# The opening of a fused attention and expert kernel: sums of squares on other engines, larger pieces, two more weight blocks converted early

## The chip, the core and the metric

The kernel runs on one core of a Trainium2 chip. What counts is the device time of one execution in microseconds, from the first to the last thing the core does. The engines are named as in the profile: PE (TensorE), DVE (VectorE), ACT (ScalarE), POOL (GpSimd) and SP (SyncE, which here only issues transfers).

## The reference

Two batches of 6016 tokens with 256 channels go through a channel attention and two dense layers. The scores contract over the tokens, so each batch has one 256 x 256 score matrix:

```python
qn = q / (np.linalg.norm(q, axis=1, keepdims=True) + 1e-06)   # norm over the 6016 tokens
kn = k / (np.linalg.norm(k, axis=1, keepdims=True) + 1e-06)
s = kn.transpose(0, 2, 1) @ qn / tau
a = softmax(s)                                                # with 1e-09 in the denominator
x = (v @ a).reshape(12032, 256)
x = (sigmoid(x @ w_gate) * (x @ w_val)) @ w_out               # d_ff 1536
h = x @ w_in
out = (h - np.tanh(h)) @ w_out2                               # d_ff 2048
```

All inputs are fp32, the weights arrive as float64 bit patterns in two 32-bit words each (seen from the kernel), and the products are done on TensorE in fp32 (S) or as pairs of fp32r halves, high and low, with three products for one.

## The kernel before

**Order of the whole.** The schedule is written out by hand: each engine executes its instructions in the order in which the Python text emits them. The opening handles batch 0's q and k, the softmax and the first weight blocks; then a list of units (24 tiles of up to 512 tokens, two layers) keeps PE busy to the end, with batch 1's scores done beside it. Only the opening is touched by the change.

**Pieces.** Each partition holds 47 rows (tokens) of q and k. `pieces` cuts them: three of 2 rows, nine of 4, then 2, 2 and 1. `qk_load` (L215) puts one transfer for q and one for k on SP's queue, into a ring of 14 buffers, so seven pieces can be in flight; the loop (L357) loads piece j + 6, then works on piece j.

**Scores and squares.** `qk_scores` (L249) multiplies each row of k, in two halves of 128 channels, with the row of q, and accumulates in one PSUM bank, S0; each product in fp32 shows as two PE instructions. `qk_squares` (L239) squares a piece on ACT into an SBUF buffer (two of these in turn) and adds it on DVE to a sum of four rows for q and one for k. `fold` (L245) adds halves of the sums until one row is left. Then PE forms the norms (`nps`, L383), a chain of small DVE and ACT steps takes the roots and inverses, PE spreads q's inverse norms over the partitions (`spread`, L403), DVE scales the scores (L276), ACT takes the exponentials (L280), and PE transposes (`turn`, L289). PE has S products of the last pieces (their second half, c = 1) behind nps, and products of batch 1 (`fill`, L232, loaded by `fill_load`, L223), to do in between.

**Weights.** Weight blocks are named wgv{f}_{jc} and wo{c}; one is 512 KB of float64 words. `convert` (L102) is a generator that turns them into fp32r halves in five steps: `load` on SP, `rebias` (L118) on ACT, `shift` (L124) and `join` (L130) on DVE, `hi` (L137) on ACT, `lo` (L142) on DVE. `join(n)` also issues load(n + ahead). `pump(n)` advances it by n yields, and so sets where its instructions stand among the others. The first stream, conv0, has two items with ahead=2: both loads are issued among the first pieces, and the steps run in the pumps of j = 5 to 7. The second stream, conv, has ahead=4 and starts at j = 9. The order of the steps is this (L149):

```python
        for n in range(lead):
            rebias(n)
        for n in range(len(items) + 2):
            if shift(n):
                yield
            ...
            for do in (lambda n: lo(n - 2), join):
                if do(n):
                    yield
            hi(n)
            if lead == 2:
                rebias(n + 2)
```

**Products of the weights.** `aw_block` (L294) multiplies a converted block with the softmax; its first use of wgv1 and wgv2 is between the first units. `ones0` is a tile of ones; `warm` products on it stand ahead of S on PE (L350).

Of the kernel before, what the change touches and what calls it, by code (L numbers as in the profile page):

```python
# [8 lines left out]
F32 = mybir.dt.float32  # L9
# [4 lines left out]
AF = mybir.ActivationFunctionType  # L14
# [3 lines left out]
P = 128  # L18
B, S, D = 2, 6016, 256
R = S // P  # L20
RP = 4
# [13 lines left out]
LATE = 8  # L35


NRAW, NYQ, WARM = 14, 1, 3


START2, DENSE = 24.3, 0.48
# [23 lines left out]
def attn_moe_kernel(  # L65
# [12 lines left out]
    nc = tc.nc  # L78
    ctx.enter_context(tc.manual_schedule())
    mm = nc.tensor.matmul  # L80
# [6 lines left out]
    sp = sctx.enter_context(tc.tile_pool(name="sp", bufs=1, reuse_waits="tile"))  # L87
# [3 lines left out]
    def ring(name):  # L91
        return pp.tile([P, CH], F32, tag="ring", bufs=4, name=name)

    def bank(tag, name):
        return pp.tile([P, CH], F32, tag=tag, name=name)
# [6 lines left out]
    def convert(pool, items, done, ahead=4, raws=4, lead=2):  # L102

        jobs = {}

        def load(n):
            if n < len(items):
                src, dst, name = items[n]  # L110
                raw = pool.tile([P, CH, 2], U32, tag="craw", bufs=raws, name=f"raw_{name}")
                nc.sync.dma_start(raw, src.bitcast(U32).rearrange("p (c two) -> p c two", two=2))
                jobs[n] = [raw[:, :, 0], raw[:, :, 1].bitcast(F32), dst, name, None, None]

        def rebias(n):
            if n in jobs:
                x = pool.tile([P, CH], U32, tag="cx", bufs=4, name=f"x_{jobs[n][3]}")
                nc.scalar.activation(x.bitcast(F32), jobs[n][1], AF.Prelu, scale=2.0**-112, alpha=-(2.0**32))  # L118
                jobs[n][4] = x

        def shift(n):
            if n in jobs:
                x = jobs[n][4]
                nc.vector.tensor_scalar(x, x, 3, 0xFFFFFFFF, op0=ALU.logical_shift_left, op1=ALU.bitwise_and)  # L124
                return True

        def join(n):
            if n in jobs:
                x = jobs[n][4]
                nc.vector.scalar_tensor_tensor(x, jobs[n][0], 29, x, op0=ALU.logical_shift_right, op1=ALU.bitwise_or)  # L130
                load(n + ahead)
                return True

        def hi(n):
            if n in jobs:
                t = jobs[n][5] = jobs[n][2]()
                nc.scalar.copy(t[:, 0], jobs[n][4].bitcast(F32))  # L137

        def lo(n):
            if n in jobs:  # L140
                _, _, _, name, x, t = jobs.pop(n)
                nc.vector.tensor_sub(t[:, 1], x.bitcast(F32), t[:, 0].bitcast(F32))  # L142
                done(name)
                return True

        for n in range(ahead):
            load(n)
# [6 lines that stand above are left out]
            if lead == 1:  # L154
                rebias(n + 1)
# [6 lines that stand above are left out]
# [3 lines left out]
    def pump(n):  # L165
        for _ in range(n):
            if stream[0] is not None and next(stream[0], 1) == 1:
                stream[0] = None


    ident = base.tile([P, P], F32, name="ident")
    ones0 = sp.tile([P, P], F32, name="ones0")
    sums = [sp.tile([P, RP, D], F32, name=f"sum{x}") for x in "qk"]
    rs = [base.tile([P, 2], F32, name=f"rs{b}") for b in range(B)]
    warm = base.tile([P, 1], F32, name="warm")
# [6 lines left out]
    def constants():  # L182
        for t in sums:
            nc.gpsimd.memset(t, 0.0)
        make_identity(nc, ident)
        nc.vector.memset(c_b, C_B)
        nc.vector.memset(c_m, -U_MAX)
        nc.gpsimd.dma_start(itau, tau.to_broadcast((P, 1)))
# [7 lines left out]
    def wgv_item(f, jc):  # L196
        return (wgv[2 * f + jc], lambda: wgv_t[f][:, :, jc, :], f"wgv{f}_{jc}")
# [1 line left out]
    def wo_item(c):  # L199
        return (wo[c], lambda: wo_t[c], f"wo{c}")  # L200

    conv0 = [wgv_item(0, jc) for jc in range(2)]
    conv = [wgv_item(1, jc) for jc in range(2)]
    for f in range(2, NW // 2):
        conv += [wo_item(f - 2), wgv_item(f, 0), wgv_item(f, 1)]
    conv += [wo_item(c) for c in range(NO - 2, NO)]
# [2 lines left out]
    qk0 = {}  # L209
    S0 = bank("o0", "S0").rearrange("p (c j) -> p c j", c=2)  # L210

    def token_rows(x, b):
        return x[b].rearrange("(p r) c -> p r c", r=R)

    def qk_load(r0, rn):  # L215
        for x, src in (("q", q), ("k", k)):
            raw = qk0[x, r0] = sp.tile([P, RP, D], F32, name=f"raw{x}{r0}", tag="raw", bufs=NRAW)
            nc.sync.dma_start(raw[:, :rn, :], token_rows(src, 0)[:, r0 : r0 + rn, :])
# [4 lines left out]
    def fill_load():  # L223
        fp = fctx.enter_context(tc.tile_pool(name="fp", bufs=1, side="right", reuse_waits="tile"))
        for r0, rn in FILL_LOADS:
            for x, src in (("q", q), ("k", k)):
                t = fp.tile([P, rn, D], F32, name=f"fill{x}{r0}")
                nc.sync.dma_start(t, token_rows(src, 1)[:, r0 : r0 + rn, :])
                for r in range(rn):
                    fq[x, r0 + r] = t[:, r, :]  # L230
# [5 lines left out]
                mm(S1[:, c], fq["k", r][:, c * P : (c + 1) * P], fq["q", r], start=r == 0 and c == 0, stop=r == sum(FILL) - 1, skip_group_check=True)  # L236
        filled[0] += FILL[g]

    def qk_squares(r0, rn):  # L239
        for x, t in zip("qk", sums):  # L240
            sq = sp.tile([P, RP, D], F32, name=f"sq{x}{r0}", tag="sq", bufs=2)[:, :rn, :]
            nc.scalar.activation(sq, qk0[x, r0][:, :rn, :], AF.Square)
            nc.vector.tensor_add(t[:, :rn, :], t[:, :rn, :], sq)

    def fold(h):  # L245
        for t in sums:
            nc.vector.tensor_add(t[:, :h, :], t[:, :h, :], t[:, h : 2 * h, :])

    def qk_scores(r0, rn, cs=(0, 1), rows=None):  # L249
        for r in rows or range(rn):  # L250
            for c in cs:
                w = qk0["k", r0][:, r, c * P : (c + 1) * P]
                mm(S0[:, c], w, qk0["q", r0][:, r, :], start=r0 + r == 0 and c == 0, stop=r0 + r == R - 1, skip_group_check=True)  # L253
# [55 lines left out]
    def load_v(i):  # L309
        if i >= NT:  # L310
            return
        b, off, _, n = tiles[i]
        t = vp.tile([P, 2, NM], F32, tag="vraw", name=f"vraw{i}")
        nc.sync.dma_start(t[:, :, :n], vT[b].rearrange("(c p) n -> p c n", p=P)[:, :, off : off + n])
        raws[i] = t
# [23 lines left out]
        while not ready.issuperset(names):  # L339
            pump(1)  # L340

    pieces = [(r0, 2) for r0 in range(0, 6, 2)] + [(r0, RP) for r0 in range(6, 42, RP)] + [(42, 2), (44, 2), (46, 1)]
    NP = len(pieces)
    AHEAD = NRAW // 2 - 1
    nc.vector.memset(ones0, 1.0)
    qk_load(*pieces[0])
    qk_load(*pieces[1])
    constants()
    for n in range(WARM):
        mm(bank("o1", f"warm{n}")[:, :P], ones0, ones0, start=True, stop=True)  # L350
    for j, pc in enumerate(pieces[2:AHEAD]):
        qk_load(*pc)
        if j == 2:
# [3 lines left out]
    for j, pc in enumerate(pieces[:-1]):  # L357
        if j + AHEAD < NP:
            qk_load(*pieces[j + AHEAD])
            if j + AHEAD == NP - 1:  # L360
                load_v(0)
        if j == NP - 3:
            fold(2)
        qk_squares(*pc)
        if 5 <= j < 8:
            pump(2)
        if j == 9:
            pump(1000)
            stream[0] = convert(stg, conv, stash)
            pump(1)  # L370
            fill_load()
        qk_scores(*pc, (0, 1) if j < NP - 4 else (0,))
        if j == NP - 4:
            qk_scores(*pc, (1,), range(2))
    fold(1)
    qk_squares(*pieces[-1])
    split_v(0, eng=nc.gpsimd)

# [7 lines left out]
    rn = sp.tile([P, 4], F32, name="rn")  # L386
# [5 lines left out]
    dq = sp.tile([P, 2, P], F32, name="dq")  # L392
# [3 lines left out]
    nc.vector.tensor_scalar_mul(rn[:, 2:4], rn[:, 2:4], itau[:, 0:1])  # L396
    pump(2)
    qk_scores(*pieces[-1], (0,))
    qk_scores(*pieces[-4], (1,), range(2, RP))
    for pc in pieces[-3:-1]:  # L400
        qk_scores(*pc, (1,))
    ps = ring("spread")
    mm(ps[:, :D], ones0, dq.rearrange("p c j -> p (c j)"), start=True, stop=True)  # L403
    qk_scores(*pieces[-1], (1,))
    rqs = sp.tile([P, D], F32, name="rqs")
    nc.scalar.copy(rqs, ps[:, :D])
    e0 = sp.tile([P, 2, D], F32, name="e0")
# [332 lines left out]
    for u in units:  # L740
        at, kind, i, c = u
# [4 lines left out]
        if kind == 1 and i == 1 and c == 2:  # L746
            t = cst.tile([P, NM], F32, name="s1_out")
# [86 lines left out]
```

## Time and profile before

| | |
|---|---|
| median of 3 runs | 2316.07 us (2316.01 to 2316.17) |
| the profiled execution's own time | 2316.01 us |
| its span, first to last instruction | 2314.2 us |
| mean granted clock of PE | 1.000 |
| busy share PE, DVE, ACT, POOL | 100%, 79%, 68%, 2% |
| first S product, first nps | 4.34 us, 44.65 us |

The span is what the trace covers; the profiled time has 1.8 us more around it. All times inside the trace are microseconds from the start of the span. The opening is the stretch up to about 62 us, where the units begin.

### The profile page before, as it was taken

The page shows a single profiled execution, that of the slowest core. Times are in us where ns is not written, and L with a number is a line of the kernel's source. Part 1 is how long each engine was busy: PE and PEld are TensorE (multiplying, and loading weights), DVE is VectorE, ACT ScalarE, POOL GpSimd, SP SyncE. Part 2 cuts the span into 40 slices and gives each one's busy share as a digit, 9 for nine tenths or more (in the row PEclk, how much of TensorE's full clock was granted, in tenths as well). Part 3 has the DMA queues.
Part 4 walks back from the last instruction along what each step waited for, and adds up shares of the span by engine and source line. Part 5 has one row for each costly group of instructions (what it writes and reads, how often), then busy time and mean ns, then how long its engine had stood idle before and what let it go on. Part 6 is the DMA issues. An engine that isn't in the chain of part 4 may idle for free.

```text
span 2314.2 us, 28241 instructions
## 1 busy us (share of the span) xinstructions
PE 2302.7 (100%) x10416; PEld 1928.2 (83%) x10416; DVE 1826.2 (79%) x2886; ACT 1578.5 (68%) x2862; POOL 48.3 (2%) x50
## 2 busy tenths in 40 slices
PE   9999999999999999999999999999999999999998
PEld 7888888888888888888888888888888888888897
DVE  7778888888888888877777777777777777777778
ACT  6567777677676767776666666666666666666667
POOL 1000000000000000000000000000000000000006
PEclk9999999999999999999999999999999999999999
DMA  9640001110101101011110000000000000000000
GB/s 367 210 133 9 20 22 37 37 37 19 37 28 32 38 19 37 0 35 37 55 37 12 6 19 10 10 19 1 19 14 5 19 10 10 19 1 17 10 1 17
DMA packets 39242, 84.65 MB, mean 37 GB/s; under 512 B 4032, under 2 KB 17344, under 8 KB 37568
## 3 DMA queue, kind: packets, MB, share of 16 engines
q1 hardware_dynamic: 38064, 76.36, 9.9%
q0 software_dynamic: 896, 6.29, 0.7%
q8 instruction: 81, 1.33, 0.2%
q14 instruction: 57, 0.47, 0.1%
q10 hardware_dynamic: 144, 0.20, 0.0%
HBM read 63.96 MB, written 18.87 MB: 36 GB/s over the span
## 4 chain that ended last, share of the span: by engine, by line
PE 95%; DVE 3%; ACT 1%; DMA 1%; issue 0%; SPq 0%; DVEq 0%; ACTq 0%
PE ps L450 11%; PE ps L449 11%; PE ps L454 11%; PE h L450 7%; PE h L454 7%; PE h L449 7%; PE o L454 7%; PE o L449 7%; PE o L450 7%; PE y L450 5%; PE y L454 5%; PE y L449 5%; PE S L253 1%; DMA rawk<-in_k_dram 1%; PE aw L300 0%
## 5 line engine op out<-in xcount | busy, mean ns | idle before, releaser
L450 PE MATMUL ps<-vhl,aw 128*128 128x512 f32 (+1 forms) x1152 | 443.6, 385 | 0.0
L449 PE MATMUL ps<-vhl,aw 128*128 128x512 f32 (+1 forms) x1152 | 443.3, 385 | 0.0
L516 DVE TENSOR_TENSOR d<-h,d 128x512 f32<-128x512 f32 (+1 forms) x368 | 251.6, 684 | 234.2 <-ACT d L512 233.6
L544 ACT CAST hl<-s 128x512 fp32r<-128x512 f32 (+1 forms) x384 | 234.8, 612 | 279.7 <-DVE s L520 274.0
L511 ACT ACTIVATE u<-h 128x512 f32<-128x512 f32 (+1 forms) x384 | 226.5, 590 | 238.2 <-PE h L454 237.8
L454 PE MATMUL ps<-vhl,aw 128*128 128x512 f32 (+1 forms) x1152 | 349.9, 385 | 0.0
L518 DVE TENSOR_TENSOR u<-h,u 128x512 f32<-128x512 f32 (+1 forms) x360 | 245.7, 683 | 112.3 <-ACT big L515 112.2
L449 PE MATMUL o<-hl,wv 128*128 128x512 f32 (+1 forms) x768 | 295.8, 385 | 1.2 <-ACT hl L544 1.2
L450 PE MATMUL h<-yhl,wi 128*128 128x512 f32 (+1 forms) x768 | 295.8, 385 | 0.0
L449 PE MATMUL h<-yhl,wi 128*128 128x512 f32 (+1 forms) x768 | 295.7, 385 | 0.0
L450 PE MATMUL o<-hl,wv 128*128 128x512 f32 (+1 forms) x768 | 295.5, 385 | 0.0
L520 DVE COPY_PREDICATED s<-big,d 128x512 f32<-128x512 int16 (+1 forms) x368 | 274.9, 747 | 13.1
L513 ACT ACTIVATE s<-u,c_b 128x512 f32<-128x512 f32 (+1 forms) x384 | 275.9, 719 | 1.9 <-DVE hl L546 1.9
L515 ACT ACTIVATE big<-u,c_m 128x512 bf16<-128x512 f32 (+1 forms) x368 | 263.5, 716 | 0.0
L519 DVE SCALAR_TENSOR_TENSOR s<-s,u 128x512 f32<-128x512 f32 (+1 forms) x360 | 247.1, 686 | 12.3
L450 PEld LDWEIGHTS ps<-vhl,aw 128*128 128x128 f32 x1152 | 216.4, 188 | 41.2
L449 PEld LDWEIGHTS ps<-vhl,aw 128*128 128x128 f32 x1152 | 216.3, 188 | 40.9
L454 PEld LDWEIGHTS ps<-vhl,aw 128*128 128x128 f32 x1152 | 215.7, 188 | 41.5
L490 DVE TENSOR_TENSOR sg<-ps,sg 128x512 f32<-128x512 f32 (+1 forms) x288 | 194.4, 675 | 70.6 <-PE ps L454 54.6
L546 DVE TENSOR_TENSOR hl<-s,hl 128x512 fp32r<-128x512 f32 (+1 forms) x361 | 243.8, 675 | 0.6 <-ACT hl L544 0.6
L454 PE MATMUL o<-hl,wv 128*128 128x512 f32 (+1 forms) x768 | 234.8, 387 | 2.2 <-POOL hl L546 1.7
L489 ACT ACTIVATE sg<-ps 128x512 f32<-128x512 f32 (+1 forms) x288 | 170.0, 590 | 98.2 <-PE ps L454 93.7
(157 smaller groups left out, 3530.6 us busy)
## 6 DMA issues: line engine op xcount, KB each, us to landing
vraw<-in_vT_dram SPq DMA_DIRECT2D x22, 512.0 KB, 3.7
out_dram<-out SPq DMA_DIRECT2D x44, 256.0 KB, 2.2
raw_wgv<-in_wgv_dram SPq DMA_DIRECT2D x12, 512.0 KB, 5.8
wgv_d<-wgv POOLq DMA_DIRECT2D x6, 1024.0 KB, 6.8
wb<-wgv_d SPq DMA_DIRECT2D x6, 1024.0 KB, 4.8
raw<-in_q_dram SPq DMA_DIRECT2D x47, 128.0 KB, 2.1
raw<-in_k_dram SPq DMA_DIRECT2D x47, 128.0 KB, 2.2
rawq<-in_q_dram SPq DMA_DIRECT2D x9, 512.0 KB, 10.2
```

Source lines behind the costliest of these rows:

```text
L449: mm(ps[:, :n], wh, xh, start=first and j == 0, stop=False)
L450: mm(ps[:, :n], wl, xh, start=False, stop=False)
L454: mm(ps[:, :n], wh, xl, start=False, stop=last and j == len(wts) - 1)
L511: nc.scalar.activation(u, H, AF.Square)
L513: nc.scalar.activation(s, u, AF.Square, scale=C_S, bias=c_b[:, 0:1])
L515: nc.scalar.activation(big, u, AF.Relu, bias=c_m[:, 0:1])
L516: nc.vector.tensor_sub(d, H, d)
L518: nc.vector.tensor_mul(w, H, u)
L519: nc.vector.scalar_tensor_tensor(s, s, C_D, w, op0=ALU.add, op1=ALU.mult)
L520: nc.vector.copy_predicated(s, big.bitcast(I16), d)
L544: nc.scalar.copy(hl[:, 0, :n], x)
L546: eng.tensor_sub(hl[:, 1, :n], x, hl[:, 0, :n].bitcast(F32))
```

## The change

- `qk_squares` gets an argument `away`. For pieces 0 to 7 (QPOOL) q's squares stay in SBUF and are added on GpSimd. All other squares are done in steps of two rows, written by ACT to a PSUM bank of the common ring of four, and added from there on DVE.
- The pieces are now one of 2 rows, ten of 4, then 2, 2 and 1: 14 in all.
- conv0 has four items, wgv0 and wgv1, and conv begins with wo0. conv0 is still opened with ahead=2. The pumps of two yields now run at j = 5 to 9, and what is left of conv0 at j = 10.
- `fill_load` comes ahead of the second stream's first loads.
- The products on constants are four of 256 columns ahead of S, and three more after piece 0 (before: three of 128 columns ahead of S). `ones0` is twice as wide.
- The second half (c = 1) of all four rows of the fourth piece from the end goes behind nps (before: two of them), and behind the spread product stand the last two pieces instead of one.

```diff
--- before.py
+++ after.py
@@ -35,7 +35,8 @@
 LATE = 8
 
 
-NRAW, NYQ, WARM = 14, 1, 3
+NRAW, NYQ, WARM = 14, 1, (4, 3)
+QPOOL = 8
 
 
 START2, DENSE = 24.3, 0.48
@@ -169,7 +170,7 @@
 
 
     ident = base.tile([P, P], F32, name="ident")
-    ones0 = sp.tile([P, P], F32, name="ones0")
+    ones0 = sp.tile([P, D], F32, name="ones0")
     sums = [sp.tile([P, RP, D], F32, name=f"sum{x}") for x in "qk"]
     rs = [base.tile([P, 2], F32, name=f"rs{b}") for b in range(B)]
     warm = base.tile([P, 1], F32, name="warm")
@@ -199,8 +200,8 @@
     def wo_item(c):
         return (wo[c], lambda: wo_t[c], f"wo{c}")
 
-    conv0 = [wgv_item(0, jc) for jc in range(2)]
-    conv = [wgv_item(1, jc) for jc in range(2)]
+    conv0 = [wgv_item(f, jc) for f in range(2) for jc in range(2)]
+    conv = []
     for f in range(2, NW // 2):
         conv += [wo_item(f - 2), wgv_item(f, 0), wgv_item(f, 1)]
     conv += [wo_item(c) for c in range(NO - 2, NO)]
@@ -236,11 +237,19 @@
                 mm(S1[:, c], fq["k", r][:, c * P : (c + 1) * P], fq["q", r], start=r == 0 and c == 0, stop=r == sum(FILL) - 1, skip_group_check=True)
         filled[0] += FILL[g]
 
-    def qk_squares(r0, rn):
+    def qk_squares(r0, rn, away=False):
         for x, t in zip("qk", sums):
-            sq = sp.tile([P, RP, D], F32, name=f"sq{x}{r0}", tag="sq", bufs=2)[:, :rn, :]
-            nc.scalar.activation(sq, qk0[x, r0][:, :rn, :], AF.Square)
-            nc.vector.tensor_add(t[:, :rn, :], t[:, :rn, :], sq)
+            raw = qk0[x, r0]
+            if x == "q" and away:
+                sq = sp.tile([P, RP, D], F32, name=f"sq{x}{r0}", tag="sq", bufs=2)[:, :rn, :]
+                nc.scalar.activation(sq, raw[:, :rn, :], AF.Square)
+                nc.gpsimd.tensor_add(t[:, :rn, :], t[:, :rn, :], sq)
+                continue
+            for r in range(0, rn, 2):
+                rs_ = slice(r, min(rn, r + 2))
+                sq = ring(f"sq{x}{r0}_{r}").rearrange("p (r c) -> p r c", c=D)[:, : rs_.stop - r, :]
+                nc.scalar.activation(sq, raw[:, rs_, :], AF.Square)
+                nc.vector.tensor_add(t[:, rs_, :], t[:, rs_, :], sq)
 
     def fold(h):
         for t in sums:
@@ -339,15 +348,19 @@
         while not ready.issuperset(names):
             pump(1)
 
-    pieces = [(r0, 2) for r0 in range(0, 6, 2)] + [(r0, RP) for r0 in range(6, 42, RP)] + [(42, 2), (44, 2), (46, 1)]
+    pieces = [(0, 2)] + [(r0, RP) for r0 in range(2, 42, RP)] + [(42, 2), (44, 2), (46, 1)]
     NP = len(pieces)
     AHEAD = NRAW // 2 - 1
     nc.vector.memset(ones0, 1.0)
     qk_load(*pieces[0])
     qk_load(*pieces[1])
     constants()
-    for n in range(WARM):
-        mm(bank("o1", f"warm{n}")[:, :P], ones0, ones0, start=True, stop=True)
+
+    def warm_up(h):
+        for n in range(WARM[h]):
+            mm(bank("o1", f"warm{h}_{n}")[:, :D], ones0[:, :P], ones0, start=True, stop=True)
+
+    warm_up(0)
     for j, pc in enumerate(pieces[2:AHEAD]):
         qk_load(*pc)
         if j == 2:
@@ -361,17 +374,17 @@
                 load_v(0)
         if j == NP - 3:
             fold(2)
-        qk_squares(*pc)
-        if 5 <= j < 8:
+        qk_squares(*pc, j < QPOOL)
+        if 5 <= j < 10:
             pump(2)
-        if j == 9:
+        if j == 10:
             pump(1000)
+            fill_load()
             stream[0] = convert(stg, conv, stash)
             pump(1)
-            fill_load()
         qk_scores(*pc, (0, 1) if j < NP - 4 else (0,))
-        if j == NP - 4:
-            qk_scores(*pc, (1,), range(2))
+        if j == 0:
+            warm_up(1)
     fold(1)
     qk_squares(*pieces[-1])
     split_v(0, eng=nc.gpsimd)
@@ -396,12 +409,12 @@
     nc.vector.tensor_scalar_mul(rn[:, 2:4], rn[:, 2:4], itau[:, 0:1])
     pump(2)
     qk_scores(*pieces[-1], (0,))
-    qk_scores(*pieces[-4], (1,), range(2, RP))
-    for pc in pieces[-3:-1]:
+    for pc in pieces[-4:-2]:
         qk_scores(*pc, (1,))
     ps = ring("spread")
-    mm(ps[:, :D], ones0, dq.rearrange("p c j -> p (c j)"), start=True, stop=True)
-    qk_scores(*pieces[-1], (1,))
+    mm(ps[:, :D], ones0[:, :P], dq.rearrange("p c j -> p (c j)"), start=True, stop=True)
+    for pc in pieces[-2:]:
+        qk_scores(*pc, (1,))
     rqs = sp.tile([P, D], F32, name="rqs")
     nc.scalar.copy(rqs, ps[:, :D])
     e0 = sp.tile([P, 2, D], F32, name="e0")
```

## Rows read from the trace of the kernel before

**Rows 1.** The page's head and part 1: busy us, share, instructions.

```profile
span 2314.2 us, 28241 instructions
...
PE 2302.7 (100%) x10416; PEld 1928.2 (83%) x10416; DVE 1826.2 (79%) x2886; ACT 1578.5 (68%) x2862; POOL 48.3 (2%) x50
```

**Rows 2.** Windows over the opening: us; busy us (instructions) of PE, PEld, DVE, ACT, POOL; PEclk; DMA share; GB/s.

```profile
30.00:40.00 10.00, 10.00 (x48) 8.81 (x47) 10.00 (x10) 7.60 (x8) 0.00 (x0) 1.00 1.04 387
```

**Rows 3.** PE in order of time: start, us, what, xcount, idle before and its releaser.

```profile
4.34 14.66 PE L253 MATMUL S<-rawq,rawk 128*128 128x256 f32 x56 [0.79 <-DMA rawk<-in_k_dram]
19.54 25.27 PE L253 MATMUL S<-rawq,rawk 128*128 128x256 f32 x116 [0.54 <-DMA rawk<-in_k_dram]
44.65 0.50 PE L383 MATMUL nps<-ones,sumq 128*128 128x2 f32 x4
45.02 0.59 PE L383 MATMUL nps<-ones,sumk 128*128 128x2 f32 x4
```

**Rows 4.** Windows of the S products on PE: us, busy (instructions), PEclk, DMA share, GB/s.

```profile
4.50:8.50 4.00, 4.00 (x10) 1.00 0.71 237
...
20.00:40.00 20.00, 20.00 (x94) 1.00 1.03 398
```

**Rows 5.** ACT in order of time.

```profile
4.23 0.63 ACT L242 ACTIVATE sqk<-rawk 128x512 f32<-128x512 f32 x1
...
8.79 0.63 ACT L242 ACTIVATE sqk<-rawk 128x512 f32<-128x512 f32 x1 [0.32 <-DMA rawk<-in_k_dram]
...
19.49 1.06 ACT L242 ACTIVATE sqk<-rawk 128x1024 f32<-128x1024 f32 x1 [0.22 <-DMA rawk<-in_k_dram]
20.45 1.23 ACT L118 ACTIVATE x_wgv<-raw_wgv 128x512 f32<-128x512 f32 x2
21.58 1.04 ACT L242 ACTIVATE sqq<-rawq 128x1024 f32<-128x1024 f32 x1
22.53 1.04 ACT L242 ACTIVATE sqk<-rawk 128x1024 f32<-128x1024 f32 x1
```

**Rows 6.** SP's queue in order of time: start and length of the issue.

```profile
5.86 2.07 SPq L112 DMA_DIRECT2D raw_wgv<-in_wgv_dram  x2
...
18.20 0.33 SPq L218 DMA_DIRECT2D rawq<-in_q_dram  x1
...
28.44 0.33 SPq L218 DMA_DIRECT2D rawq<-in_q_dram  x1
```

**Rows 7.** DVE in order of time.

```profile
43.38 0.42 DVE L243 TENSOR_TENSOR sumq<-sumq,sqq 128x256 f32<-128x256 f32 x1
43.71 0.41 DVE L243 TENSOR_TENSOR sumk<-sumk,sqk 128x256 f32<-128x256 f32 x1
...
65.82 0.69 DVE L490 TENSOR_TENSOR sg<-ps,sg 128x512 f32<-128x512 f32 x1 [0.80 <-ACT sg L489]
66.43 0.68 DVE L130 SCALAR_TENSOR_TENSOR x_wgv<-raw_wgv,x_wgv 128x512 uint32<-128x512 uint32 x1
67.03 0.42 DVE L124 TENSOR_SCALAR x_wo<-x_wo 128x512 uint32<-128x512 uint32 x1
67.36 0.69 DVE L142 TENSOR_TENSOR wgv<-x_wgv,wgv 128x512 fp32r<-128x512 f32 x1
```

**Rows 8.** GpSimd and DVE in order of time, and the page's usual duration.

```profile
43.83 2.65 POOL L100 TENSOR_TENSOR vhl<-vraw,vhl 128x512 fp32r<-128x512 f32 x2 [40.03 <-ACT vhl L99]
...
2266.63 1.29 POOL L546 TENSOR_TENSOR hl<-s,hl 128x512 fp32r<-128x512 f32 x1 [3.12 <-PE h L450]
...
2267.10 1.42 DVE L520 COPY_PREDICATED s<-big,d 128x512 f32<-128x512 int16 x1
...
L520 DVE COPY_PREDICATED s<-big,d 128x512 f32<-128x512 int16 (+1 forms) x368 | 274.9, 747 | 13.1
```

**Rows 9.** PE before the second turn, and PE's waits for conversions (total, times, longest).

```profile
52.19 0.44 PE L289 MATMUL turn<-ident,e 128*128 128x128 f32 x2 [0.35 <-ACT e L280]
...
PE aw L300 <- DVE wgv L142: 1.0, 2, 0.6
```

## The prediction

> **What bounds the kernel now.** I read the page first. TensorE (PE) is busy 2302.7 of 2314.2 us [rows 1], so time can only be won where PE waits or runs slowly, and only lost where it is made to wait. The change edits the opening alone, so I went there by ten-microsecond windows, then through PE, ACT, SP and DVE in order of time.
>
> PE starts the products S at 4.34. The first 56 instructions take 14.66 us, the next 116 take 25.27 us without a gap, and the norm products nps begin at 44.65, directly behind them [rows 3]. The pace changes on the way: ten instructions in 4 us at first, 94 in 20 us later, so 0.43 us each and then 0.21 to 0.22 us [rows 4]. The granted clock reads 1.00 in both stretches, but the pace is that of 1.2 and of 2.4 GHz.
>
> DVE is just as full: 10.00 of 10 us between 30 and 40, with the DMA engines at a share of 1.04 [rows 2]. Its last sum ends at 43.71 + 0.41 = 44.12 [rows 7], half a microsecond before PE asks for it. So three things run level in the opening: the transfers, the sums of squares on DVE, and PE. Whatever makes the sums late by more than half a microsecond moves nps, and with it all that follows.
>
> The transfers come in the order in which SP issues them. The two weight loads are issued at 5.86, behind fourteen rows of q and k [rows 6]; the fifth piece after them lands at 19.49 [rows 5], and PE waits 0.54 us for it [rows 3]. From 18.20 to 28.44 SP can issue only once in 1.28 us [rows 6], whenever one of the 512 KB transfers ahead has drained: 0.64 us for one row of q with its k (256 KB).
>
> **What the change can win.** The 56 first instructions at the fast pace are 12.2 us, not 14.66; with the waits of 0.54, of 0.35 before the second turn, and of 1.0 in two places for the conversion of a weight block [rows 9], all that can be had in the opening is 2.5 + 0.5 + 0.4 + 1.0 = 4.4 us, 0.19% of the kernel. 0.2% (4.6 us) is about what a measurement of this kernel can tell from no change.
>
> **Where it loses: the third weight block.** The converter still runs with two loads ahead, but now has four items. Its third load is issued inside join(0), in the pump of j = 5. On SP that is behind the loads of pieces 0 to 11, 44 rows. Its consumer, rebias(2), stands on ACT in the pump of j = 6, in front of the squares of pieces 7 to 13. ACT takes its instructions in order, as its rows do everywhere here [rows 5]. So ACT stops after piece 6 until a transfer lands that is queued five pieces further on. Behind ACT wait DVE's sums and GpSimd's, and behind those nps and all of PE.
>
> When it lands: before, 18 rows and two blocks were there at 19.49. The third block needs 26 more rows and itself: 19.49 + 26 x 0.64 + 1.28 = 37.4. Four-row pieces speed up the start: before, rows 3 to 6 came between 4.23 and 8.79 [rows 5], 4.6 us for what takes 2.6 at the later rate. That gives 0 to 2.0 us; I take 1.2, since part of that delay is the start of the queue itself. The landing is at 36.2, in bounds of 35.4 to 37.4. Piece 6 lands at 19.49 + 2 x 2.56 - 1.2 = 23.4, so ACT stands some 11 us.
>
> What then remains, with L for the landing:
> - ACT does rebias(2) (0.57, from two in 1.23), the square of q of piece 7 (0.95, start to start) and the first half of k (0.6) [rows 5]: DVE can begin its sums at L + 2.2.
> - DVE then has 18 sums of 512 elements. The new ones read one operand from PSUM; the nearest row that does so advances in 0.61 [rows 7]. Taken as 0.60: 10.8 us. The last row's two take 0.33 each (0.7), the folds 2 x 0.6 and 2 x 0.33 (1.9), two shifts 0.33 (0.7), two joins and four subtractions 0.6 each (3.6) [rows 7]. Together 17.7 us. ACT's own list to the end is some 15 us (18 halves at 0.6, the rest 4.4), so DVE ends last. Squares written to PSUM are not in the trace; between 0.5 and 0.65 each they stay under DVE.
> - GpSimd adds q of piece 7 from about L + 1.6. Two adds of 512 took 2.65 [rows 8], so it ends at L + 4.2. The shift of DVE comes up at L + 3.4. One row shows what happens then: GpSimd ran from 2266.63 to 2267.92, a DVE instruction with SBUF operands that started at 2267.10 took 1.42 instead of the usual 0.75, to 0.60 after GpSimd's end [rows 8]. I add 0.8 us; the bounds are 0 and 2.6.
>
> The port rule for this is in the Trainium skill (SBUF — State Buffer, "Who interferes with whom"): VectorE with two SBUF inputs or in a two-port mode and GpSimd exclude one another for a whole instruction, while a sum with one input in PSUM is not held. By that the 18 sums run free beside GpSimd, as I have them, and the shift pays the 0.8; without any lock the forecast would be 2328.9. Row and rule agree.
>
> The sums end at 36.2 + 2.2 + 17.7 + 0.8 = 56.9. The norm products of k, at 45.02 before [rows 3], start at about 56.9: **+11.9 us.**
>
> **What else moves.**
> - GpSimd takes q's sums of pieces 0 to 7, 30 rows. Some 2.6 us for a piece of four rows is as fast as one lands (2.56), and DVE folds long after: nothing. Without the stall this is what frees DVE.
> - Four more S instructions (two rows, one half) are moved behind nps: +0.9 us after it, since before it PE now only waits.
> - PE has done its S at about 42 to 44 and then stands some 13 us. The trace has no such wait: after idle times up to 0.6 the pace stays fast; after the start, which is nearer, ten instructions ran at half pace [rows 4], 10 x 0.21 = 2.1 us. I take 2.1, bounds 0 and 2.1.
>
> The Trainium skill (TensorE: Matmul & The Clock Gate, "HAM oscillation — how this bites in real kernels") says that a long wait between bursts puts the engine back to half clock, which would give the 2.1; no wait here is long enough to show it.
>
> - The extra products on constants (four of 256 columns before S, three after piece 0) fall into time that PE later waits away: nothing. Without the stall they cost 6 x 0.22 to 6 x 0.43 us if piece 1 is there by then.
> - The second weight block is ready early, so the two waits for conversion go: -1.0. The six S instructions behind the spread product cover part of the wait before the turn: -0.2 (0 to 0.4).
> - The fill loads now stand ahead of the second stream's loads on SP: four blocks land some 6 us later, but their first use is after the softmax, which is 12 us later. Nothing. v's first tile and its split follow the last squares and are needed 15 us on: nothing.
>
> Sum: 11.9 + 0.9 + 2.1 - 1.2 = **+13.7 us.** The profiled execution took 2316.01 for a span of 2314.2, and the median is 2316.07, so **2329.7 us**, 0.59% slower. By the bounds: low -0.8 (landing) -0.8 (no lock) -2.1 (clock) -0.2 = 2325.8; high +1.2 (landing) +1.4 (18 sums from PSUM at their full 0.69 [rows 7], with no overlap) +1.2 (nothing saved later) = 2333.5.
>
> **The rivals.**
> - *The third block is not late* (it lands by about L = 23, so that L + 20.7 meets nps at 44): it would have to pass 20 rows issued ahead of it. Against this stands that the first two blocks took their turn, piece 5 behind them being late by just their 2.6 us. Then the opening is only smoothed: nps comes at 42.4 (fast clock from the start) to 44.1 (as late as before), against 44.65, +0.9 for the moved S, -1.2 later: -0.9 to -2.6, so 2313.4 to 2315.1, no change that can be told. Chance 0.07.
> - *Faster by over 0.2%*: needs all of the 4.4 us above and more: 2311.4. It decides only if every wait of the opening goes and no S runs at half pace. Chance 0.02.
> - *Partly late*: a faster start and DVE emptying its list while ACT waits on load three; the delay at nps falls to some 5 us: 2319 to 2323. For it speaks only that my count of DVE's list rests on rows at full load. Chance 0.08; half of it is below 2320.7.
> - *GpSimd becomes the bound*: its adds blocked by DVE's conversions in the early pieces, and ACT held by the two buffers of q. Eight adds are some 20 us from 5.7; they would have to end after L + 15 to decide, and the stall gives them 11 us of peace. Worth under 2 us on top, 2331. Chance 0.03.
>
> My case has 0.80. **Range:** 2323 to 2335, its own bounds with room for the partly late case below and a longer half-pace stretch above. Faster 0.02, within 0.2% 0.11, slower 0.87.
>
> **What the profile will show.** ACT idle for 10 to 12 us before the Prelu of the third block (raw_wgv), released by a DMA at 35 to 37.5; DVE idle with it, then full until about 57; PE without work from 42 to 44 until nps at 56 to 57.5, then S at 0.43 us for some instructions; no wait of PE for wgv around 72. I am wrong if the third block lands in the twenties, if ACT's squares of pieces 7 and on run ahead of that Prelu, or if the sums after the landing take much less than 20 us.

## The result, and the profile after

The changed kernel takes **2334.58 us** (median of 5 runs, 2333.97 to 2336.85) against 2316.07: ratio 1.0082, 95% interval 1.0071 to 1.0093, so 0.8% slower. The forecast was 2329.7, slower by 13.6 us; it is slower by 18.5. The direction and the place are the ones forecast, the size is not: the median lies at the upper end of the range (2323 to 2335), and by the ratio the time is 2335.1, just above it. The profiled execution took 2335.75 for a span of 2334.0, 19.8 us longer than the span before; the terms below are made against that pair.

ACT first, in order of time (start, length, what, count, idle before and its releaser), where the stall was forecast:

```profile
9.57 1.12 ACT L251 ACTIVATE sqk<-rawk 128x512 f32<-128x512 f32 x2 [0.24 <-DMA rawk<-in_k_dram]
...
17.42 1.12 ACT L251 ACTIVATE sqk<-rawk 128x512 f32<-128x512 f32 x2 [0.22 <-DMA rawk<-in_k_dram]
...
26.75 0.60 ACT L138 CAST wgv<-x_wgv 128x512 fp32r<-128x512 f32 x1
37.91 0.67 ACT L119 ACTIVATE x_wgv<-raw_wgv 128x512 f32<-128x512 f32 x1 [10.56 <-DMA raw_wgv<-in_wgv_dram]
38.49 1.04 ACT L245 ACTIVATE sqq<-rawq 128x1024 f32<-128x1024 f32 x1
```

ACT is done with piece 6 at 27.3 and waits 10.56 us for the third weight block; the squares of piece 7 start at 38.49. Here row 6's k comes at 9.57, against 8.79 before [rows 5]. Single executions scatter by as much: with two-row pieces five kernels had row 6 at 8.35 to 9.64, with four-row pieces nine had it at 8.80 to 9.62. The eighteenth row tells more. It came at 17.35 to 18.50 in those nine, and at 16.77 and 17.20 in the two kernels with two-row pieces that load it ahead of the weights. The four-row pieces do not speed up the start.

DVE in order of time, first a fold (`fold` adds two halves of a sum) of the kernel before, then the changed kernel from the landing to the end of the sums:

```profile
42.70 0.42 DVE L247 TENSOR_TENSOR sumq<-sumq 128x256 f32<-128x256 f32 x1
```

```profile
40.05 1.28 DVE L252 TENSOR_TENSOR sumk<-sumk,sqk 128x512 f32<-128x512 f32 x2 [10.73 <-ACT sqk L251]
41.25 1.07 DVE L125 TENSOR_SCALAR x_wgv<-x_wgv 128x512 uint32<-128x512 uint32 x1
...
47.10 1.29 DVE L252 TENSOR_TENSOR sumq<-sumq,sqq 128x512 f32<-128x512 f32 x2 [0.85 <-ACT sqq L251]
...
57.90 1.47 DVE L256 TENSOR_TENSOR sumq<-sumq 128x256 f32<-128x256 f32 x1
59.29 1.48 DVE L256 TENSOR_TENSOR sumk<-sumk 128x256 f32<-128x256 f32 x1
...
61.02 0.41 DVE L252 TENSOR_TENSOR sumk<-sumk,sqk 128x256 f32<-128x256 f32 x1
```

GpSimd in the same stretch:

```profile
39.67 2.37 POOL L246 TENSOR_TENSOR sumq<-sumq,sqq 128x1024 f32<-128x1024 f32 x1 [11.37 <-ACT sqq L245]
57.82 2.67 POOL L101 TENSOR_TENSOR vhl<-vraw,vhl 128x512 fp32r<-128x512 f32 x2 [15.78 <-ACT vhl L100]
```

The reader is to see two things. DVE is full from 40.05 to 61.43 but for 0.85 us, and the last sum ends 17.3 us later than before [rows 7]. And three of its instructions are too long: the shift at 41.25 takes 1.07 instead of 0.42 [rows 7], the two folds 1.47 and 1.48 instead of 0.42, and all three lie beside an addition or subtraction of GpSimd.

PE in order of time, to be held against [rows 3], which go on like this in the kernel before:

```profile
45.46 3.27 PE L253 MATMUL S<-rawq,rawk 128*128 128x256 f32 x14
48.57 0.59 PE L403 MATMUL spread<-dq,ones 128*128 128x256 f32 x2
```

The changed kernel:

```profile
1.19 5.06 PE L361 MATMUL warm<-ones 128*128 128x256 f32 x8 [1.19 <-DVE c_m L188]
6.04 2.64 PE L262 MATMUL S<-rawq,rawk 128*128 128x256 f32 x8
8.52 2.11 PE L361 MATMUL warm<-ones 128*128 128x256 f32 x6
10.47 34.70 PE L262 MATMUL S<-rawq,rawk 128*128 128x256 f32 x160
61.24 0.99 PE L396 MATMUL nps<-ones,sumq 128*128 128x2 f32 x4 [16.08 <-DVE sumq L252]
62.09 0.99 PE L396 MATMUL nps<-ones,sumk 128*128 128x2 f32 x4
62.95 6.25 PE L262 MATMUL S<-rawq,rawk 128*128 128x256 f32 x14
69.03 0.60 PE L415 MATMUL spread<-dq,ones 128*128 128x256 f32 x2
...
73.51 0.44 PE L298 MATMUL turn<-ident,e 128*128 128x128 f32 x2 [0.41 <-ACT e L289]
```

PE stands 16.08 us in front of nps. Behind it the fourteen S instructions take 6.1 us, to 69.03, for 3.1 before. The windows (us; busy us of PE, PEld, DVE, ACT, POOL; PEclk; DMA share; GB/s) show why:

```profile
45.00:61.00 16.00, 0.16 (x1) 0.00 (x0) 15.15 (x24) 9.57 (x18) 3.18 (x3) 0.61 0.51 201
61.00:69.00 8.00, 7.76 (x22) 6.59 (x23) 3.35 (x14) 2.81 (x5) 0.55 (x2) 0.50 0.89 329
69.00:82.00 13.00, 12.57 (x58) 10.14 (x57) 7.36 (x17) 8.51 (x18) 0.00 (x0) 1.00 0.35 122
```

The granted clock is 0.50 from 61 to 69, the level of 1.2 GHz, and 1.00 again from 69.

### The profile page after: what moved, and what is told of

It reads as the page before. It is cut to its first block, busy times and chain, and to the rows that moved or that the text cites. A ratio compares the mean times of both kernels' runs of the same rounds, so it can differ in the third digit from the quotient of the medians.

```text
span 2334.0 us, 28286 instructions
## 1 busy us (share of the span) xinstructions
PE 2308.8 (99%) x10424; PEld 1934.2 (83%) x10424; DVE 1821.8 (78%) x2889; ACT 1578.2 (68%) x2873; POOL 66.1 (3%) x58
## 4 chain that ended last, share of the span: by engine, by line
PE 94%; DVE 3%; DMA 2%; ACT 1%; issue 1%; DVEq 0%; SPq 0%; ACTq 0%
PE ps L463 11%; PE ps L467 11%; PE ps L462 11%; PE h L463 7%; PE o L467 7%; PE h L467 7%; PE h L462 7%; PE o L463 7%; PE o L462 7%; PE y L463 5%; PE y L467 5%; PE y L462 5%; DMA raw_wgv<-in_wgv_dram 1%; DMA rawq<-in_q_dram 1%; PE aw L309 0%
```

## The experiments

Twelve kernels ran, in three groups, each group beside runs of the kernel before on the same chip. The diffs are against the changed kernel, or against the kernel before where the text says so. Where executions of one kernel differ by more than a microsecond, the range stands behind the median.

**One part alone: four blocks, on the kernel before.** Squares, pieces and constants stay as before.

```diff
-    conv0 = [wgv_item(0, jc) for jc in range(2)]
-    conv = [wgv_item(1, jc) for jc in range(2)]
+    conv0 = [wgv_item(f, jc) for f in range(2) for jc in range(2)]
+    conv = []
...
-        if 5 <= j < 8:
+        if 5 <= j < 10:
             pump(2)
-        if j == 9:
+        if j == 10:
```

> The kernel before with one part of the change alone: four blocks in the opening's converter, with its pumps at j = 5 to 10; squares, pieces and constants as before. Theory (a third load queued behind 42 rows stops ACT, whatever the squares do): ACT waits to about 36, the sums end at 60 to 63, PE waits 16 us and pays half pace, total 2333 to 2338. Rival (the stall costs this much only together with the other parts): 2325 or less.

Measured: 2333.77 us, ratio 1.0075 (1.0058 to 1.0092). This one part gives 17.7 of the 18.5 us. ACT in order of time:

```profile
23.87 0.60 ACT L137 CAST wgv<-x_wgv 128x512 fp32r<-128x512 f32 x1
38.00 0.67 ACT L118 ACTIVATE x_wgv<-raw_wgv 128x512 f32<-128x512 f32 x1 [13.53 <-DMA raw_wgv<-in_wgv_dram]
```

PE in order of time:

```profile
61.64 1.01 PE L383 MATMUL nps<-ones,sumq 128*128 128x2 f32 x4 [16.44 <-DVE sumq L243]
...
63.36 5.75 PE L253 MATMUL S<-rawq,rawk 128*128 128x256 f32 x14
```

ACT waits 13.53 us, PE 16.44 us, as in the changed kernel. The squares are not needed for the loss. The rival falls.

**That part undone: two blocks.**

```diff
-    conv0 = [wgv_item(f, jc) for f in range(2) for jc in range(2)]
-    conv = []
+    conv0 = [wgv_item(0, jc) for jc in range(2)]
+    conv = [wgv_item(1, jc) for jc in range(2)]
```

> The changed kernel with only the two weight blocks of before in the opening's converter. Theory (the late third block stops ACT): no wait of 10 us on ACT, the sums end before PE has done its S, nps at about 45.2 where S ends in the changed kernel, total 2316.5 to 2318. Rival (the new way of the squares, over PSUM and GpSimd, or the four-row pieces are what costs): still 2328 or more, since all of that stays.

Measured: 2322.02 us (2321.67 to 2323.78), ratio 1.0027 (1.0017 to 1.0037). The long wait of ACT is gone and 12.6 us with it, but 6 us are left where the theory allowed 2. PE, then DVE, then GpSimd, in order of time:

```profile
48.29 0.58 PE L396 MATMUL nps<-ones,sumq 128*128 128x2 f32 x4 [2.48 <-DVE sumq L252]
...
49.17 4.96 PE L262 MATMUL S<-rawq,rawk 128*128 128x256 f32 x14
```

```profile
29.13 2.72 DVE L131 SCALAR_TENSOR_TENSOR x_wgv<-raw_wgv,x_wgv 128x512 uint32<-128x512 uint32 x1
...
44.94 1.46 DVE L256 TENSOR_TENSOR sumq<-sumq 128x256 f32<-128x256 f32 x1
46.33 1.48 DVE L256 TENSOR_TENSOR sumk<-sumk 128x256 f32<-128x256 f32 x1
```

```profile
26.43 4.87 POOL L246 TENSOR_TENSOR sumq<-sumq,sqq 128x1024 f32<-128x1024 f32 x2 [1.10 <-ACT sqq L245]
```

The sums still end 2.5 us behind PE's S. A join takes 2.72 us beside GpSimd's adds of pieces 6 and 7, the folds 1.46 and 1.48; and behind a wait of only 2.48 us the fourteen S take 4.8 us. So my account lacked two things, GpSimd's hold on DVE outside the one place I had named, and a clock that can fall after a short wait.

**The loads early, all four blocks kept.**

```diff
-            stream[0] = convert(stg, conv0, stash, ahead=2)
+            stream[0] = convert(stg, conv0, stash, ahead=4)
```

> The changed kernel with all four blocks loaded ahead of piece 5 (ahead=4 for the first stream); the same conversions at the same places. Theory (it is the place of the third and fourth load, not the work of two more blocks): ACT waits once for piece 5, to about 25, and not for the third block; nps at 45.5 to 47, the conversion waits of PE gone, total 2316 to 2319. Rival (the conversions of two more blocks overload DVE in the opening): nps at 50 or later, total 2322 or more.

Measured: 2327.03 us, ratio 1.0048 (1.0031 to 1.0064); 7.6 us less than the changed kernel. With nps at 53.76 this is the rival's case, though the place of the load has its share. PE in order of time:

```profile
25.61 20.96 PE L262 MATMUL S<-rawq,rawk 128*128 128x256 f32 x96 [1.27 <-DMA rawk<-in_k_dram]
53.76 0.98 PE L396 MATMUL nps<-ones,sumq 128*128 128x2 f32 x4 [7.19 <-DVE sumq L252]
```

ACT no longer waits for the third block. Piece 5 is late instead, by two more blocks, PE waits 1.27 us for it, and then DVE is full from 26.2 to 53.9 but for 1.3 us. So the place of the third load accounts for 7.5 us of nps (61.24 to 53.76). Two more blocks in the opening, even when they are loaded early, account for 5.5 (53.76 against 48.29 with two blocks): their conversions on DVE, and piece 5 coming 2.5 us later; the runs do not part these. The other 3.6 us, from 44.65, stand with two blocks as well.

**v's split behind the norms.** The changed kernel with one line moved:

```diff
     qk_squares(*pieces[-1])
-    split_v(0, eng=nc.gpsimd)
...
     pump(2)
+    split_v(0, eng=nc.gpsimd)
     qk_scores(*pieces[-1], (0,))
```

> The changed kernel with the split of v's first tile issued after the small chain of norms instead of ahead of it. Theory (the two folds of 1.47 and 1.48 us wait for GpSimd's two subtractions): folds back at 0.42 us, nps 2.2 us earlier, total about 2332.4. Rival (the folds are slow because GpSimd wrote the sum, or because of the backlog): folds stay at 1.5 us and the total at 2334.6.

Measured: 2333.45 us (2333.29 to 2334.30), 1.1 us less by the medians. DVE, then PE, in order of time:

```profile
57.93 0.42 DVE L256 TENSOR_TENSOR sumq<-sumq 128x256 f32<-128x256 f32 x1
58.27 0.42 DVE L256 TENSOR_TENSOR sumk<-sumk 128x256 f32<-128x256 f32 x1
```

```profile
59.16 0.98 PE L395 MATMUL nps<-ones,sumq 128*128 128x2 f32 x4 [13.27 <-DVE sumq L252]
```

The folds are back at 0.42 us and nps starts 2.1 us earlier, as the theory said. The gain in the medians is half of that; the profiled spans differ by 2.5 us (2334.0 and 2331.5). Executions of the changed kernel differ by 2.9 us among themselves, so the cause rests on the trace, and the gain in time is known to about a microsecond only.

**PE kept busy, twice.** Products on constants between S and nps, 32 and 21 of them:

```diff
+    for n in range(32):        # 21 in the second kernel
+        mm(bank("o1", f"busy{n}")[:, :D], ones0[:, :P], ones0, start=True, stop=True)
     nps = ring("nps")
```

> The changed kernel with 32 more products on constants (64 instructions, some 14 us at the fast pace) between the last S ahead of nps and nps, in the time in which PE waits. Theory (the wait of 16 us puts PE at half pace, and the nps and 14 S behind it pay): nps to S start takes 0.8 instead of 1.7 us, 14 S take 3.1 instead of 6.1 us, total 3.9 us less, about 2330.7. Rival (the chain of norms on DVE and ACT sets the spread product anyway): total within 1 us of 2334.6.

> The changed kernel with 21 products on constants between S and nps (42 instructions, 15.8 us at the 0.376 us seen for them there, ending at about 60.8, ahead of the sums at 61.4). Theory (the long wait of PE costs half pace behind it): nps to S in 0.8 us, 14 S in 3.1 us, total 3.9 us less than the changed kernel's 2334.6, so 2330.7. Rival (the chain of norms on DVE and ACT sets the spread product anyway): within 1 us of 2334.6.

Measured: 2338.99 (2338.83 to 2340.02) and 2333.89 us (2331.59 to 2335.01). Both totals miss. PE of the first, in order of time:

```profile
44.77 24.05 PE L393 MATMUL busy<-ones 128*128 128x256 f32 x64
68.66 0.50 PE L398 MATMUL nps<-ones,sumq 128*128 128x2 f32 x4
...
69.47 3.27 PE L262 MATMUL S<-rawq,rawk 128*128 128x256 f32 x14
```

A product on constants took 0.376 us per instruction, not 0.22, so 32 of them push nps 7.4 us back. But then nps to S takes 0.81 and the fourteen S 3.11 us (to 72.58) at a granted clock of 1.00: together 3.9 us less than in the changed kernel, which is what the half pace costs there. The second kernel ended its products 1.2 us ahead of the sums, and its profiled execution still shows half pace behind that wait (14 S in 4.5 us, granted 0.68); its fastest execution lies 3.0 us under the changed kernel's median. The cost of the clock is shown by the first; that filler ending a microsecond early saves it is not.

**Both repairs, and then the constants of before.** Two blocks and the late split together; and the same with three products of 128 columns:

```diff
-NRAW, NYQ, WARM = 14, 1, (4, 3)
+NRAW, NYQ, WARM = 14, 1, (3, 0)
...
-            mm(bank("o1", f"warm{h}_{n}")[:, :D], ones0[:, :P], ones0, start=True, stop=True)
+            mm(bank("o1", f"warm{h}_{n}")[:, :P], ones0[:, :P], ones0[:, :P], start=True, stop=True)
```

> Both repairs on the changed kernel: two weight blocks in the opening's converter as before, and v's first split issued after the chain of norms. Theory (what is left over 2316 with two blocks is DVE's folds waiting for GpSimd, and PE at half pace after its wait of 2.5 us): sums end at 46.4, within 0.6 us of the end of PE's S, no half pace after nps; 2322.0 - 2.1 - 1.7 = 2318.2. Rival (the rest comes from the squares' new way or the pieces): 2321 or more.

> The same with the products on constants of before (three of 128 columns ahead of S, none after piece 0). Theory (they cost PE 1.5 us, but DVE's sums end last by then): S ends 1 us earlier, nps where the sums end, total 0 to 0.5 us less than with the new ones. Rival (the new ones bring the fast clock earlier and so help): 0.5 us or more slower.

Measured: 2319.81 us (2317.79 to 2320.66; ratio 1.0012, 1.0003 to 1.0022) and 2318.78 us (2318.03 to 2319.38; ratio 1.0011, 1.0001 to 1.0020). The sums end where forecast, nps at 46.42 and 45.76. The first total is 1.6 us over its forecast and under the rival's 2321, since half pace came all the same. PE of the first, then of the second, in order of time:

```profile
46.42 0.58 PE L395 MATMUL nps<-ones,sumq 128*128 128x2 f32 x4 [1.27 <-DVE sumq L252]
...
47.31 4.95 PE L262 MATMUL S<-rawq,rawk 128*128 128x256 f32 x14
```

```profile
9.20 34.77 PE L262 MATMUL S<-rawq,rawk 128*128 128x256 f32 x160 [1.30 <-DMA rawk<-in_k_dram]
45.76 0.58 PE L395 MATMUL nps<-ones,sumq 128*128 128x2 f32 x4 [1.78 <-DVE sumq L252]
...
46.64 3.27 PE L262 MATMUL S<-rawq,rawk 128*128 128x256 f32 x14
```

With the old constants S is dense from 9.20 instead of 10.46, but nps waits for DVE in both, so it gains only what DVE's start gains. In the profiled execution of the first the fourteen S took 4.8 us after a wait of 1.27 us (granted clock 0.64 from 47.3 to 52), in the second 3.1 after one of 1.78 (1.00). By the medians the old constants are 1.0 us faster, by the ratios hardly at all, and the first kernel's executions differ by 2.9 us. So the new constants are not seen to help, and whether they cost anything is not settled.

**The other parts alone.** The squares' new way on the kernel before; and the pieces and the moved S on it (the changed kernel with two blocks, old constants and the old `qk_squares`):

```diff
-        qk_squares(*pc)          # kernel before
+        qk_squares(*pc, j < QPOOL)
```

> The kernel before with the squares' new way alone: q of pieces 0 to 7 added on GpSimd, the others over PSUM in steps of two rows. Theory (DVE's conversions wait for GpSimd's adds, 2.7 us once with two blocks, which eats most of what DVE is relieved of): a join of over 2 us in the trace, sums end at 45 to 46 instead of 44.1, total 2317 to 2319. Rival (the relief of DVE is larger): sums end ahead of PE's S, total 2316 or less.

> The changed kernel with two blocks, the constants and the squares of before: what is left is the four-row pieces and the S products moved behind nps and the spread product. Theory (these cost little): sums end at 44 to 44.5, total 2316 to 2317. Rival (the later first pieces and the moved S are what is left of the loss in the repaired kernel): 2318 or more.

Measured: 2320.26 us (2317.88 to 2321.95; ratio 1.0018, 1.0009 to 1.0027) and 2317.57 us (2317.06 to 2320.17; ratio 1.0007, 0.9998 to 1.0016). DVE and GpSimd of the first, in order of time:

```profile
25.21 2.72 DVE L131 SCALAR_TENSOR_TENSOR x_wgv<-raw_wgv,x_wgv 128x512 uint32<-128x512 uint32 x1
...
43.42 1.46 DVE L256 TENSOR_TENSOR sumq<-sumq 128x256 f32<-128x256 f32 x1
44.81 1.48 DVE L256 TENSOR_TENSOR sumk<-sumk 128x256 f32<-128x256 f32 x1
```

```profile
43.34 2.67 POOL L101 TENSOR_TENSOR vhl<-vraw,vhl 128x512 fp32r<-128x512 f32 x2 [15.95 <-ACT vhl L100]
```

The squares alone cost 4.2 us, 1.3 over the upper end of what I expected. GpSimd takes 26 rows of q off DVE, and the sums end 2.8 us later than before. The join of 2.72 was foreseen; the folds were not. In the kernel before ACT's last squares wait for DVE, since two buffers hold them, and so v's split, at 43.83 [rows 8], comes after the folds, which start at 42.70 and 43.04. With four PSUM banks ACT runs ahead, the split reaches GpSimd at 43.34, and the folds wait for it. The two other kernels with the old squares bear this out: with four blocks alone the split starts at 61.62, behind folds at 60.49 and 60.83, with the pieces alone at 44.93, behind folds at 43.80 and 44.13, and all four folds take 0.42 us. Behind its wait of 2.29 us the first kernel also pays for the clock: its fourteen S take 4.6 us, at a granted 0.66. The pieces and the moved S cost 1.5 us, between the theory's 2317 and the rival's 2318, with an interval that reaches to nothing.

**Versions that were to beat both.** On the kernel before: the first two loads one piece later; and four blocks, each pair loaded ahead of the piece at whose squares it is converted whole, with GpSimd adding q of pieces 6, 7, 9 and 10 only (all other squares over PSUM), and the second stream begun at j = 10, behind `fill_load`:

```diff
-        if j == 2:
+        if j == 3:
             stream[0] = convert(stg, conv0, stash, ahead=2)
...
-        if 5 <= j < 8:
+        if 6 <= j < 9:           # first kernel
             pump(2)
...
-        qk_squares(*pc)
+        qk_squares(*pc, j in (6, 7, 9, 10))   # second kernel
+        if j == 2:               # second kernel: conv1 is wgv1
+            second = convert(stg, conv1, stash, ahead=2)
+            next(second)
+        if j == 5:
+            pump(1000)
+        if j == 8:
+            stream[0] = second
+            pump(1000)
```

> The kernel before with the first two weight blocks loaded one piece later (behind piece 5) and converted one piece later. Theory (transfers land in the order of issue, so piece 5 comes 2.6 us earlier): PE's wait of 0.54 us at 19 goes, total 0.5 us less, 2315.5. Rival (DVE's sums end last by then): 2316.0.

> A repaired form on the kernel before: four blocks in the opening, but each pair loaded ahead of the piece at which it is converted (behind pieces 5 and 8) and converted whole in the gap that it leaves (after the squares of pieces 5 and 8); squares the new way, with GpSimd adding q of pieces 6, 7, 9 and 10 only, where no conversion runs. Theory (place of loads and of conversions is all that was wrong with early blocks): no wait of ACT above 3 us, nps at 44.1 to 44.6, PE's conversion waits of 1.0 us gone, total 2314.3 to 2315. Rival (DVE cannot hold four blocks and the sums by 44): 2317 or more.

Measured: 2316.09 us (ratio 1.0000, 0.9991 to 1.0009) and 2320.94 us (2319.16 to 2321.97; ratio 1.0020, 1.0011 to 1.0029). In the first PE's wait of 0.54 us is gone, but nps starts at 44.48 where it was at 44.65: from 8.5 to 12 PE got through 13 S instructions instead of 16, more of them at the slow pace. PE's waits for conversions grow from 1.0 to 1.4 us, and nothing is left. DVE of the second, in order of time:

```profile
27.68 1.28 DVE L252 TENSOR_TENSOR sumq<-sumq,sqq 128x512 f32<-128x512 f32 x2 [1.14 <-POOL sumq L246]
...
38.87 1.29 DVE L252 TENSOR_TENSOR sumq<-sumq,sqq 128x512 f32<-128x512 f32 x2 [1.19 <-POOL sumq L246]
...
44.86 1.46 DVE L256 TENSOR_TENSOR sumq<-sumq 128x256 f32<-128x256 f32 x1
```

No wait of ACT of the old kind is left (1.4 us for a piece is the longest), and still the sums end at 48.4: DVE waits 1.14 and 1.19 us for GpSimd's sum of q, and the folds again run into v's split. Neither beats the kernel before.

## Why the forecast had the mechanism and missed the size

The chain was the one forecast: the third load behind 44 rows on SP, `rebias(2)` ahead of the squares on ACT, DVE's list behind them, nps and PE behind DVE. Four blocks alone reproduce it. The step that failed is in the sum: v's split, put at nothing, cost DVE 2.1 us; the landing was mis-sized by 1.7 us, the clock by 1.3. All three erred on the same side. The terms, in the profiled pair:

| term | forecast | measured |
|---|---|---|
| third block there, ACT goes on | 36.2 | 37.91 |
| from there to DVE's first sum | 2.2 | 2.1 |
| DVE's list, first sum to the end of the sums | 18.5 | 21.4 |
| from there to the norm products of k | 0 | 0.7 |
| norm products of k (45.02 before) | 56.9, +11.9 | 62.09, +17.1 |
| half pace behind nps | +2.1 | +3.4 |
| all that is later | -0.3 | -0.7 |
| sum | +13.7 | +19.8 |

- **The landing, 1.7 us short.** I credited the four-row pieces with 1.2 us at the start. In this pair they cost 0.5: the fifth piece's k, row 18, came at 17.42, where the old order without weights would have it at 14.38 + 2.56 = 16.9. The step "Four-row pieces speed up the start" is wrong, and the block landed 0.5 us behind the bound of 37.4. (The piece at 19.49 is the first behind the two weight loads, not the fifth; the sum takes it rightly, as row 18.) From row 18 on the arithmetic of 0.64 us a row holds to the tenth (19.49 + 17.9 + 0.5 = 37.9), in the three other kernels with this stall too. With four blocks alone it gives 36.5 (19.87 + 24 x 0.64 + 1.28) for a measured 38.0; where these 1.5 us come from is open.
- **DVE's list, 2.9 us short.** The 18 sums at 0.60 and the blocked shift (0.7 over, for my 0.8) were right. "v's first tile and its split follow the last squares and are needed 15 us on: nothing" is the term that failed: I asked when the split is needed, and not whom it holds up. It cost the two folds 2.1 us; with the split moved they are 0.42 again. The remaining 0.85 us is DVE's wait at 47.10 for squares that stand behind a cast on ACT.
- **The clock, 1.3 us short.** I let ten instructions run at half pace, as after the start [rows 4]. All fourteen did, and the norm products with them (62.09 to 62.95, 0.86 us, for 0.44 before; 14 S 3.0 us longer). The products on constants that leave no wait take 3.9 us out from nps to the spread product, the part before the norms of k included. Waits far shorter than I thought of cost something too: fourteen S took 4.6 us behind one of 7.19 (four blocks, loaded early) and 4.8 behind one of 1.27.
- **Later.** The conversion waits of PE went, as forecast; the wait at the second turn did not (0.41 us for 0.35): DVE's scaling of the scores waits for all S products, so S behind the spread product hide nothing.
- **The rivals.** The third block was later than my latest bound, so the two rivals of an earlier one are out; GpSimd was not the bound, but its hold on DVE was dearer than the one place that I priced.

The Trainium skill (SBUF — State Buffer, "Who interferes with whom") has the rule that covers the folds: an instruction of VectorE with two SBUF inputs contends with one of GpSimd that reads SBUF, and whichever comes second is fully held. The trace agrees beyond the case for which I cited it: folds of 1.47 for 0.42, a join of 2.72 for 0.69, sums with one input in PSUM at 0.60 start to start beside GpSimd as without.

For the clock, the Trainium skill (TensorE: Matmul & The Clock Gate, "HAM oscillation — how this bites in real kernels") says that a long wait between bursts puts the engine back to half clock. The trace agrees: the wait of 16.08 us is followed by a granted clock of 0.50.

The parts do not add up: 17.7 + 4.2 + 1.5 alone, 18.5 together. My reading, which no run tests by itself: where DVE's list after a stall sets the end, what GpSimd takes off it is a relief, and what PE loses at the start is waited away.

## What to carry to other kernels

A load is late by all that stands ahead of it on its queue, and its consumer stops everything behind it on its own engine: when a generator with a fixed look-ahead gets more items, count the bytes between the issue of each load and the place of its first use. Work moved to GpSimd is not free for DVE: give GpSimd's instructions and DVE's instructions on SBUF operands different times (folds, joins and a shift were held here), and when a buffer ring gets deeper, look again at what now runs early. Of anything "needed much later", ask also what it blocks when it comes early.

## What the runs showed of the hardware that was not expected

- Half pace came after short waits as well. Behind PE waits of 1.21, 1.27, 2.29, 2.48, 3.54 and 7.19 us in six kernels the granted clock over the fourteen S was 0.64 to 0.68; behind 13.27 and 16.08 us it was 0.50; behind 1.78 us in another kernel it stayed at 1.00. What decides is not settled by these runs. In the first 8.5 us the records show 1.00 while S runs at 0.43 us an instruction.
- A product on constants into one bank, each a tile of its own, took 0.376 us an instruction at the granted clock of 1.00, against 0.217 for S, and 0.6 at the start (8 in 5.06 us); why is not shown. The seven products of the changed kernel delay S to 6.04 and its dense run to 10.47; with the three old ones and the same pieces these are 4.32 and 9.20.
- 512 KB transfers did not fill the start faster than 256 KB ones: the first eighteen rows of q and k were there at 17.35 to 18.50 us with one two-row piece ahead (nine kernels), at 16.77 and 17.20 with three (two kernels).
